# A pooled-attention and GELU kernel: denominators moved ahead of outputs in the first batch, one load moved to another queue, last row tile in two column parts

## The chip, the core and the metric

One core of a Trainium2 chip. The metric is the device time of one execution in microseconds (us), some 1.8 us longer than the span of the core's own instructions, which is what the profile shows. Engines in the profile: PE is TensorE, DVE VectorE, ACT ScalarE, POOL the gpsimd engine, SP the sync engine. Kernels are compared only within the same rounds. Ratios are the mean time of one kernel's fast runs over that of the other's of the same rounds, so not quite the ratio of the medians that are quoted; the range in brackets after a ratio is its 95% interval. Where a landing is given as a sum, it is the time of issue plus the time from issue to landing.

## The reference, cut to what matters

```python
# q, k, v: [8 batches, 8 heads, 576 rows, 64]; float32
k_p = k.reshape(B, H, 72, 8, D).mean(axis=3)         # pooled by 8
v_p = v.reshape(B, H, 72, 8, D).mean(axis=3)
attn = softmax(scale * q @ k_p^T)                    # over the 72 pooled rows
x = (attn @ v_p).transpose(0, 2, 1, 3).reshape(4608, 512)
out = gelu_tanh(x @ w_in) @ w_out                    # w_in 512 x 2048, w_out 2048 x 512
```

## The kernel before

Batch 0's attention runs alone. After that, tokens are handled in 9 groups of 512: first projection with w_in (16 blocks of 4 matmuls, each followed by a GELU on ACT), then second projection with w_out (4 row tiles of 16 matmuls), in which the scores and outputs of the next batch are put in between. Matmul operands are bfloat16. The loads of w_in, w_out and q cast from float32 and are issued by the gpsimd engine; batch 1's k and v go the same way, without a cast. One queue, in this order:

```python
    load_k(0, [nc.sync, nc.scalar])
    load_v(0, [nc.sync, nc.scalar])
    load_q(0, 0, 1); load_q(0, 1, 2)          # gpsimd queue from here on
    ...
    load_w_in(0); load_w_in(1)
    load_k(1, [nc.gpsimd])
    load_q(1)
    load_v(1, [nc.gpsimd])                    # two halves: heads 0-3 to partitions 0-63, heads 4-7 to 64-127
    for i in range(4): ...                    # w_out in four quarters
```

The end of batch 0's attention. `den0` sums exponentials on PE, `inverse0` makes 1/sum on ACT, `av0` is the output product on PE, `mult0` scales it on DVE; the last argument is the first of the banks used of PSUM, the memory that matmuls write to. `spin` issues matmuls on zeros, results unused, which keep PE busy while it waits for ACT and DVE:

```python
    inverse0(1, 0, 6)
    spin(4, 4)
    av0(0, 0, 4); mult0(0, 0, 4)
    den0(0, 2, 2); inverse0(0, 2, 2)
    av0(1, 0, 0); mult0(1, 0, 0)
    spin(3, 6)
    den0(1, 2, 6); inverse0(1, 2, 6)
    spin(3, 4)
    av0(0, 2, 4); mult0(0, 2, 4)
    spin(3, 0)
    av0(1, 2, 0); mult0(1, 2, 0)
    for fo, ko in [(fo, ko) for ko in range(2) for fo in range(4)]:
        p1_mm(0, fo, ko)                      # group 0's first projection starts
```

In group 0, work for batch 1 hangs on the blocks of the first projection; `kk` are the sums over k on DVE, `tq` the four groups of q's transposes on PE, `tk` k's transposes, `vv` the sums over v. Then each row tile of the second projection is copied out of PSUM and stored with four DMAs:

```python
    plan = {0: kk, 12: tq[:1], 13: tq[1:2] + tk, 14: tq[2:3], 15: tq[3:] + vv}
    ...
    nc.vector.tensor_copy(out=osb, in_=PS[:, o_bank(g, r), :])
    for n in range(4): ...                    # 32 rows each; on sync, every other one on scalar for the last tile
```

The softmax here doesn't subtract the row's maximum and nothing guards it: scores larger than these inputs give would overflow.

## Time and profile before

| | before |
|---|---|
| device time, median of 4 | 309.03 us (308.62 to 309.35) |
| the profiled execution | 308.29 us, span 306.5 us |
| PE busy | 298.2 us, 97% of the span |
| ACT, DVE, POOL busy | 71%, 49%, 12% |
| HBM read, written | 36.70 MB, 9.44 MB |

PE is busy nearly throughout, so a gain must shorten PE's work, a wait of PE, or what follows its last matmul. The profiled execution was faster than any of the timed ones. The prediction shows the views that carry this.

### The profile page before, as it was taken

Reading aid. Unit: us, or ns where it says so; the run is one execution under the profiler, and the core shown is the slowest. Engines: PE = TensorE matmul, PEld = TensorE weight load, DVE = VectorE, ACT = ScalarE, POOL = GpSimd, SP = SyncE. Lnnn points to the kernel's source line nnn. Section 1 sums busy time; section 2 is a strip of 40 time slices with the busy share of each in tenths; the row PEclk is TensorE's granted clock in tenths of the full one; section 3 lists DMA queues with packets and bytes.
Section 4 is the critical chain, followed back from the end, with each engine's and each line's share of the span. In section 5 each row is a group of like instructions: output and inputs, shape, how many; then the busy total and the mean of one; then the engine's idle time right before and its main releaser. Section 6 shows DMA issues by size and latency. Waiting matters only on the chain.

```text
span 306.5 us, 4325 instructions
## 1 busy us (share of the span) xinstructions
PE 298.2 (97%) x1518; PEld 157.4 (51%) x1548; DVE 150.4 (49%) x334; ACT 219.0 (71%) x402; POOL 36.3 (12%) x69
## 2 busy tenths in 40 slices
PE   8999999999999999999999999999999999999994
PEld 3555555555555555555555555555555555445441
DVE  5868557573677057806681559245933630110021
ACT  1686679868987798779977998789868987206400
POOL 7103002305004000220014000400000000000000
PEclk9999999999999999999999999999999999999999
DMA  7999996987957952596159725662101210121022
GB/s 225 266 257 253 214 186 137 299 176 177 269 146 167 247 122 51 114 282 156 34 112 266 168 56 106 200 151 71 35 1 36 63 41 2 34 70 34 2 70 68
DMA packets 30359, 41.12 MB, mean 134 GB/s; under 512 B 18113, under 2 KB 18113, under 8 KB 29441
## 3 DMA queue, kind: packets, MB, share of 16 engines
q0 software_dynamic: 7856, 25.43, 34.9%
q1 hardware_dynamic: 21888, 14.09, 19.2%
q10 hardware_dynamic: 592, 1.31, 1.2%
q8 instruction: 12, 0.20, 0.3%
q14 instruction: 11, 0.08, 0.1%
HBM read 36.70 MB, written 9.44 MB: 151 GB/s over the span
## 4 chain that ended last, share of the span: by engine, by line
PE 83%; DMA 12%; POOL 1%; issue 1%; ACT 0%; DVE 0%; POOLq 0%
PE PS L345 38%; PE PS L336 36%; DMA kt<-in_k_dram 7%; DMA w_out_b<-in_moe_w_out_dram 5%; PE PS L239 4%; PE PS L261 4%; PE PS L174 1%; POOL w_in_b L105 0%; POOL qb L86 0%; POOL w_out_b L113 0%; DVE osb L350 0%; ACT e L247 0%; ACT ld L269 0%; ACT ld L268 0%; POOL identb masks.py:199 0%
## 5 line engine op out<-in xcount | busy, mean ns | idle before, releaser
L345 PE MATMUL PS<-w_out_b,gT 128*128 128x512 bf16 x560 | 134.2, 379 | 0.9
L336 PE MATMUL PS<-xT,w_in_b 128*128 128x512 bf16 x563 | 126.2, 379 | 0.6
L342 ACT ACTIVATE gT<-PS 128x512 bf16<-128x512 f32 x144 | 81.1, 604 | 47.5 <-PE PS L336 47.4
L336 PEld LDWEIGHTS <-w_in_b 128*128 128x128 bf16 x576 | 64.7, 113 | 57.2
L345 PEld LDWEIGHTS <-gT 128*128 128x128 bf16 x576 | 56.1, 97 | 56.7 <-issue 1.1
L350 DVE COPY osb<-PS 128x512 f32<-128x512 f32 x36 | 24.9, 691 | 98.3 <-PE PS L345 95.3
L279 DVE TENSOR_TENSOR xT<-PS,rc 64x288 bf16<-64x288 f32 x112 | 51.0, 455 | 31.6 <-ACT rc L271 29.3
L247 ACT ACTIVATE e<-PS 72x576 bf16<-72x576 f32 (+1 forms) x64 | 41.0, 646 | 9.1 <-PE PS L239 8.2
L239 PE MATMUL PS<-qT,kT 128*72 128x288 bf16 (+1 forms) x128 | 25.9, 286 | 0.9 <-ACT qT L214 0.6
L271 ACT ACTIVATE rc<-ld 128x288 f32<-128x288 f32 x56 | 24.8, 443 | 1.8
L314 ACT ACT_TABLE_LOAD x17 | 21.8, 1283 | 4.3 <-issue 4.1
L268 ACT ACTIVATE ld<-PS 64x288 f32<-64x288 f32 x56 | 22.8, 407 | 1.3
L269 ACT ACTIVATE ld<-PS 64x288 f32<-64x288 f32 x56 | 22.5, 402 | 1.3
L261 PE MATMUL PS<-e,vp 72*128 72x288 bf16 (+1 forms) x112 | 23.1, 286 | 0.0
L139 DVE TENSOR_TENSOR kt<-kt 128x1280 f32<-128x1280 f32 (+5 forms) x18 | 18.8, 1044 | 5.5 <-DMA kt<-in_v_dram 2.6
L239 PEld LDWEIGHTS <-kT 128*72 128x72 bf16 (+1 forms) x128 | 13.2, 105 | 15.2 <-DVE qT L216 1.2
L448 POOL COPY gate<-qT 1x2 bf16<-1x2 bf16 x6 | 1.0, 174 | 140.0 <-DMA qT<-qb 140.0
L139 DVE TENSOR_TENSOR vt<-vt 128x1024 f32<-128x1024 f32 (+1 forms) x16 | 15.3, 956 | 1.8 <-DMA vt<-in_v_dram 1.5
L184 DVE COPY kT<-PS 64x288 bf16<-64x288 bf16 (+2 forms) x48 | 13.0, 319 | 6.2 <-PE PS L174 6.1
L362 PE MATMUL PS<-idle 128*128 128x512 bf16 x39 | 11.9, 447 | 1.2 <-DVE idle L127 1.2
L261 PEld LDWEIGHTS <-vp 72*128 72x128 bf16 (+1 forms) x112 | 11.0, 98 | 3.8
L81 POOL DMA_DIRECT2D vt<-in_v_dram x14 | 9.0, 655 | 7.5 <-DMA w_in_b<-in_moe_w_in_dram 5.5
(47 smaller groups left out, 90.0 us busy)
## 6 DMA issues: line engine op xcount, KB each, us to landing
out_dram<-osb SPq DMA_DIRECT2D x142, 64.0 KB
kt<-in_k_dram POOLq DMA_DIRECT2D x7, 1024.0 KB, 6.2
vt<-in_v_dram POOLq DMA_DIRECT2D x14, 512.0 KB, 8.6
qb<-in_q_dram POOLq DMA_DIRECT2D x7, 576.0 KB, 11.6
w_in_b<-in_moe_w_in_dram POOLq DMA_DIRECT2D x2, 1024.0 KB, 16.7
w_out_b<-in_moe_w_out_dram POOLq DMA_DIRECT2D x4, 512.0 KB, 13.9
kt<-in_k_dram POOLq DMA_DIRECT2D x7, 128.0 KB, 5.9
kt<-in_v_dram POOLq DMA_DIRECT2D x14, 64.0 KB, 5.7
```

The lines of the kernel that those rows point to most:

```text
L139: nc.vector.tensor_tensor(out=o, in0=a, in1=b, op=ALU.add)
L239: nc.tensor.matmul(out=PS[:n, bank + e, :CH].rearrange("j (t p) -> j t p", p=32), lhsT=kTs[b % 2][c][:, h, :n], rhs=qTs[b][:, h // 4, :, h ...
L247: nc.scalar.activation(out=e[:n], in_=PS[:n, bank:bank + 2, :CH], func=ACT.Exp, scale=1.0 / 64.0)
L261: nc.tensor.matmul(out=PS[:, bank + x, :CH], lhsT=window(vps[b % 2][:n], 2 * pr + x), rhs=e[:n, x, :], start=True, stop=True)
L268: nc.scalar.activation(out=ld[0:64], in_=PS[64:128, bank, :CH], func=ACT.Ln)
L269: nc.scalar.activation(out=ld[64:128], in_=PS[0:64, bank + 1, :CH], func=ACT.Ln)
L271: nc.scalar.activation(out=rc, in_=ld, func=ACT.Exp, scale=-1.0)
L279: nc.vector.tensor_tensor(out=xT[rows, pr, col:col + CH], in0=PS[rows, bank + x, :CH], in1=rc[rows], op=ALU.mult)
L336: nc.tensor.matmul(out=PS[:, h_bank(g, fo), c0:c1], lhsT=w_in_b[fo // 8][:, ko, q * 512 + j:(q + 1) * 512:4], rhs=xT[:, ko, r0 + c0:r0 + c ...
L342: nc.scalar.activation(out=gTs[g][:, fo, :], in_=PS[:, h_bank(g, fo), :], func=ACT.Gelu_apprx_tanh)
L345: nc.tensor.matmul(out=PS[:, o_bank(g, r), :], lhsT=gTs[g][:, fo, r * 128:(r + 1) * 128], rhs=w_out_b[:, fo, :], start=(fo == 0), stop=(fo ...
L350: nc.vector.tensor_copy(out=osb, in_=PS[:, o_bank(g, r), :])
```

## The change

Three parts. The later denominators go ahead of the outputs, so that ACT gets them sooner and fewer zero matmuls are needed (six for thirteen in the stretch shown). Batch 1's v goes to the sync queue, issued after a one-column memset of its tile on DVE that follows the first product; so it moves beside w_in, k and q instead of behind them. The last row tile is computed, copied and stored in columns 0:384 and then 384:512.

```diff
-    load_v(1, [nc.gpsimd])
...
-    spin(4, 4)
+    spin(2, 4)
+    den0(0, 2, 2)
+    inverse0(0, 2, 2)
+    spin(2, 4)
     av0(0, 0, 4)
     mult0(0, 0, 4)
-    den0(0, 2, 2)
-    inverse0(0, 2, 2)
+
+    nc.vector.memset(vts[1][:, 0, 0:1], 0.0)
+    load_v(1, [nc.sync])
+    den0(1, 2, 6)
+    inverse0(1, 2, 6)
     av0(1, 0, 0)
     mult0(1, 0, 0)
-    spin(3, 6)
-    den0(1, 2, 6)
-    inverse0(1, 2, 6)
-    spin(3, 4)
     av0(0, 2, 4)
     mult0(0, 2, 4)
-    spin(3, 0)
+    spin(2, 0)
...
-        seq = [(r, fo) for r in range(4) for fo in range(FO)]
+        seq = [(r, fo) for r in range(4 if g + 1 < NG else 3) for fo in range(FO)]
...
+    for c0, c1, bank in ((0, 384, o_bank(g, 3)), (384, DM, 4)):
+        for fo in range(FO):
+            p2_mm(g, 3, fo, bank, c0, c1)
+        store(g, 3, bank, c0, c1)
```

More of the change, by code (lines that the diff above doesn't have):

```diff
@@ L342, in gelu, with p2_mm, store @@
         nc.scalar.activation(out=gTs[g][:, fo, :], in_=PS[:, h_bank(g, fo), :], func=ACT.Gelu_apprx_tanh)
-    def p2_mm(g, r, fo):
-        nc.tensor.matmul(out=PS[:, o_bank(g, r), :], lhsT=gTs[g][:, fo, r * 128:(r + 1) * 128], rhs=w_out_b[:, fo, :],
-                         start=(fo == 0), stop=(fo == FO - 1))
-    def store(g, r):
-        osb = opool.tile([128, DM], F32, name="osb")
-        nc.vector.tensor_copy(out=osb, in_=PS[:, o_bank(g, r), :])
+    def p2_mm(g, r, fo, bank, c0=0, c1=DM):
+        nc.tensor.matmul(out=PS[:, bank, c0:c1], lhsT=gTs[g][:, fo, r * 128:(r + 1) * 128],
+                         rhs=w_out_b[:, fo, c0:c1], start=(fo == 0), stop=(fo == FO - 1))
+    osbs = {}
+    def store(g, r, bank, c0=0, c1=DM):
+        if (g, r) not in osbs:
+            osbs[g, r] = opool.tile([128, DM], F32, name="osb")
+        osb = osbs[g, r]
+        nc.vector.tensor_copy(out=osb[:, c0:c1], in_=PS[:, bank, c0:c1])
         for n in range(4):
-            b, c = divmod(g * GROUP + r * 128 + n * 32, S)
+            b, col = divmod(g * GROUP + r * 128 + n * 32, S)
             rows = out[b * S:(b + 1) * S].rearrange("(p t e) d -> e t p d", t=TP, e=2)
-            eng = nc.scalar if (g, r) == (NG - 1, 3) and n % 2 else nc.sync
-            eng.dma_start(out=rows[c // CH, c % CH // 32], in_=osb[n * 32:(n + 1) * 32, :])
+            eng = nc.scalar if c1 - c0 < DM and n % 2 else nc.sync
+            eng.dma_start(out=rows[col // CH, col % CH // 32, :, c0:c1], in_=osb[n * 32:(n + 1) * 32, c0:c1])
     def spin(n, bank):
@@ L519 @@
                 f(*a)
-            p2_mm(g, r, fo)
+            p2_mm(g, r, fo, o_bank(g, r))
             if fo == FO - 1:
-                store(g, r)
+                store(g, r, o_bank(g, r))
         for m in sorted(todo):
```

## The prediction

> **What bounds the kernel now.** I read the page first: busy shares, then the slices. TensorE (PE) carries the span.
>
> ```profile
> PE 298.2 (97%) x1518; PEld 157.4 (51%) x1548; DVE 150.4 (49%) x334; ACT 219.0 (71%) x402; POOL 36.3 (12%) x69
> ...
> PE   8999999999999999999999999999999999999994
> ...
> PEclk9999999999999999999999999999999999999999
> ```
>
> PE has no slack from the second slice to the last one, and its clock is granted in full. So time is saved only by taking instructions off PE, by removing a wait that PE still has, or by shortening what follows its last matmul. The change touches two stretches, about 16 to 45 us and the end, so I read those closely. First PE's timeline where the zero matmuls (line 362) stand:
>
> ```profile
> 15.98 1.03 PE L362 MATMUL PS<-idle 128*128 128x512 bf16 x4
> 17.18 0.66 PE L304 MATMUL PS<-e,vz 72*128 72x288 bf16 x4 [0.17 <-DVE vz L139]
> 17.68 0.66 PE L289 MATMUL PS<-e,ones 128*128 128x288 bf16 x4
> 18.17 0.66 PE L304 MATMUL PS<-e,vz 72*128 72x288 bf16 x4
> 18.66 0.81 PE L362 MATMUL PS<-idle 128*128 128x512 bf16 x3
> 19.31 0.65 PE L289 MATMUL PS<-e,ones 128*128 128x288 bf16 x4
> 19.80 0.81 PE L362 MATMUL PS<-idle 128*128 128x512 bf16 x3
> 20.45 0.65 PE L304 MATMUL PS<-e,vz 128*128 128x288 bf16 x4
> 20.94 0.81 PE L362 MATMUL PS<-idle 128*128 128x512 bf16 x3
> 21.59 0.65 PE L304 MATMUL PS<-e,vz 128*128 128x288 bf16 x4
> 22.08 0.38 PE L336 MATMUL PS<-xT,w_in_b 128*128 128x512 bf16 x1
> ```
>
> Starts are what counts, as matmuls overlap: three zero matmuls advance PE by 0.65 us (18.66 to 19.31), 0.216 each; four 288-column ones by 0.49. The zero matmuls fill time in which ScalarE and VectorE make the denominators and products; the first real projection starts at 22.08.
>
> Next, the chain that ended last, in order of time. Before group 0's second projection it is no PE chain but a DMA chain:
>
> ```profile
> 27.46 16.53 DMA w_out_b<-in_moe_w_out_dram
> 43.99 0.04 issue
> 44.03 0.81 PE PS L345 x3
> ```
>
> The last quarter of w_out lands at 43.99 and PE starts at once. Counting from the block that starts at 42.94, the fifth matmul (the first that needs this quarter) was due at 42.94 + 4 x 0.216 = 43.80, so PE waited 0.2 us. The block at 40.94 hides a like 0.2 us (its six matmuls take 1.51 us where 1.29 is due). Loading and PE are thus within 0.2 us of each other here: **PE time saved before 44 us is worth nothing unless w_out comes earlier.** That is the main question. The DMA view, two us of the startup, four us while batch 1's v moved, and four of w_out alone:
>
> ```profile
> q10 hardware_dynamic: 124, 0.25, 35.5%
> ...
> q0 software_dynamic: 239, 0.85, 105.8%
> ...
> q0 software_dynamic: 233, 0.84, 104.5%
> ```
>
> Columns are packets, MB and share of the 16 engines' time. The first row is ScalarE's hardware queue from 11 to 13 us, when only batch 0's v was left on it: 0.25 MB in 35.5% of 2 us is 352 GB/s of engine time. The second is the gpsimd queue from 29 to 33 us with batch 1's v in it: 0.85 MB in 4.23 us of engine time is 201 GB/s, like the casting w_out load of the third row (37 to 41 us), though v is not cast. In the software queue v costs the engines as much as a casting load. The engines are full from 3 to 45 us.
>
> **What the Trainium skill says.** "TensorE: Matmul & The Clock Gate", section "Back-to-back issue gap", gives N/2.4 + 2.5 ns warm, 216 ns for 512 columns and 56 for 128. The trace agrees: 0.216 above, and five 128-column transposes at 33.30 advance PE by 0.28 us. "DMA: Bandwidth & Descriptors", section "Issuing engines are not separate DMA queues", says that another issuing engine saves only sequencer time, as all share 16 engines. The trace does not quite agree: 352 against 201 GB/s for the same kind of v load. The same page, "Queues, rings and completion order", says that each DMA engine serves its queues in turn, packet by packet. It agrees with 5 to 13 us, where the three queues moved about 100 packets each in every two us. So v on the sync queue will not wait behind w_in, k and q; it will slow them.
>
> **Part 1, the order and seven zero matmuls fewer.** Thirteen of them follow 15.98 in four blocks (4, 3, 3, 3); the change keeps six (2, 2, 2). By PE time: 7 x 0.216 = 1.51 us. What of it becomes waiting? I put the new order on the old durations. Two zeros end at 16.41; the denominators (their second exponential was done by 15.7) to 16.90; two zeros to 17.33; outputs (0,0) to 17.83 (vz ready at 17.12, so the 0.17 us wait is gone); denominators (1,2) to 18.32; outputs (1,0) to 18.81. VectorE multiplies (0,0) from about 18.0 to 18.8 (0.76 each), does a tiny memset, and multiplies (1,0) until about 19.8. Outputs (0,2) need the banks of the first product: 18.9 to 19.4. The last two zeros write the bank that (1,0)'s product reads, so they wait until 19.8: 0.4 us idle. Then 0.43 to 20.25 and 0.49 to **20.75**. The third product ends at 20.5 and the fourth, whose inverse ScalarE ends at about 20.8, at 21.6, before the ninth projection matmul needs it (20.75 + 8 x 0.216 = 22.5). So the projection starts 22.08 - 20.75 = **1.33 us** earlier. The first half of w_in landed by 17.5 (3.04 + 14.2 by its tile view), so it does not hold this.
>
> **Part 2, v on the sync queue.** The issue follows the memset, near 19.0, and bytes flow from about 20.1 (1.1 us after issue, as at the start). v is 1.05 MB: at 352 GB/s 3.0 us of engine time, at the old 201 to 213 about 5. So w_out, behind it in both cases, lands about 2 us earlier: 43.99 to about 42.0. PE will want the last quarter at 43.80 - 1.33 = 42.5. The DMA bound goes, and with it the 0.4 us of waiting. But what lay before v is now delayed by up to 3.0 us: the second half of w_in from 23.0 (3.8 + 19.2) to at most 25, wanted at 20.75 + 32 x 0.216 = 27.7, harmless; k from 26.1 to about 28.8, where VectorE gets to it at 28.4 now and PE transposes the result only at 34.67, harmless. And batch 1's q:
>
> ```profile
> DMA to landing us min/median/max: 7.1/9.1/21.7
> ```
>
> This is the q tile's view up to 25 us, three loads; the slowest is batch 1's, issued at 8.59, so it lands at 30.3. PE transposes it at 33.30 now and wants it at 31.97 then. With 2 to 3 us added it lands at 32.3 to 33.3: I choose 32.8, a new wait of **0.8 us**. So this stretch keeps 1.33 - 0.8 + 0.4 = **0.9 us** (0.4 to 1.75). From then on PE is dense, and the gain goes through to the end.
>
> **Part 3, the last tile in columns 0:384 and 384:512.** The end now:
>
> ```profile
> 302.11 0.69 DVE L350 COPY osb<-PS 128x512 f32<-128x512 f32 x1 [2.76 <-PE PS L345]
> 302.83 0.78 SPq L356 DMA_DIRECT2D out_dram<-osb  x2
> 302.84 0.85 ACTq L356 DMA_DIRECT2D out_dram<-osb  x2
> ```
>
> Sixteen more matmuls, but the same columns: 16 x (0.162 + 0.056) against 16 x 0.216 is +0.03 us. The last copy has 128 columns: 0.69 is 0.53 at one element a cycle of 0.96 GHz plus 0.16, so 0.13 + 0.16 = 0.29, saving 0.40. The first part's copy (0.56) and its four issues run from about 301.3 to 302.6, so the second part's can go out at about 302.5 to 302.65 instead of 302.83; with 16 KB instead of 64 KB each the last landing comes 0.4 to 0.7 us earlier. I take **0.5 us**. "VectorE: DVE Perf Modes", section "Why PSUM operands drop a tier", keeps float32 from PSUM at one element a cycle, which 0.69 us for 512 columns fits.
>
> **Sum.** 0.9 + 0.5 = 1.4, and a little for the chance that q comes in time: 1.6 us. 309.19 - 1.6 = 307.6 us.
>
> **Rivals.** (a) Loading stays the bound: v costs 5 us on the sync queue too, w_out still lands at 44.0. For it: full DMA engines and the skill's sentence. Against it: 352 GB/s on the hardware queue. Then the start gives about 0.1 and the end 0.5: 308.6. (b) q comes in time, because v takes fewer turns before it: the start gives 1.33 + 0.4, the whole 2.2: 307.0. (c) The new order makes ScalarE or the banks the wait, and PE idles for the removed zeros; 1.33 falls to 0.5 or less, but then q's wait shrinks as well: about 308. (d) Less activity lowers the PE clock; gaps of 0.4 us beside a dense stream speak against it, and I give it little.
>
> **Range and chances.** Rival (a) and the three runs before (308.62 to 309.35) set the upper edge, 308.8; (b) with some noise the lower, 306.7. Two per cent is 6.2 us, over three times the best sum and far from any loss I can find: faster 0.01, same 0.98, slower 0.01.
>
> **What would show it.** First projection matmul near 20.75; PE waiting up to 1.3 us at the transposes of batch 1's q after 13 of the 16 blocks; last quarter of w_out before 42.5 and no wait on it; batch 1's v on the sync queue at some 350 GB/s; last copy near 0.29 us, and about 3.9 us instead of 4.4 (306.5 - 302.1) from the last matmul to the span's end. A q wait above 1.5 us, w_out still at 44, or a projection start after 21.5 would make me wrong; so would a slower dense part.

## The result

The changed kernel took 307.45 us (median of 4, 306.73 to 307.9) against 309.03; ratio 0.9947, 95% interval 0.9924 to 0.9971. That is the same within 2%, and 1.6 us faster. A second measurement (below) gave 307.13 against 309.04, ratio 0.9942.

The profile of the changed kernel, in the order of the prediction. PE's timeline over the reordered stretch (start us, us, engine, line, operation, operands, count; in brackets what PE waited for):

```profile
16.11 0.59 PE L365 MATMUL PS<-idle 128*128 128x512 bf16 x2
16.54 0.65 PE L288 MATMUL PS<-e,ones 128*128 128x288 bf16 x4
17.03 0.59 PE L365 MATMUL PS<-idle 128*128 128x512 bf16 x2
17.46 0.66 PE L303 MATMUL PS<-e,vz 72*128 72x288 bf16 x4
17.95 0.66 PE L288 MATMUL PS<-e,ones 128*128 128x288 bf16 x4
18.44 1.24 PE L303 MATMUL PS<-e,vz 72*128 72x288 bf16 x8
20.02 0.59 PE L365 MATMUL PS<-idle 128*128 128x512 bf16 x2 [0.34 <-DVE xT L307]
20.45 0.65 PE L303 MATMUL PS<-e,vz 128*128 128x288 bf16 x4
20.94 1.24 PE L335 MATMUL PS<-xT,w_in_b 128*128 128x512 bf16 x5
```

The order is as worked out, with one wait of 0.34 us for the product that reads the bank of the last zeros (0.4 predicted). The projection starts at 20.94 (20.75 predicted) instead of 22.08. What comes before this stretch also varies from trace to trace, so the better measure counts from the first zero matmul: 22.08 - 15.98 = 6.10 us before, 20.94 - 16.11 = 4.83 after, 1.27 us less.

Next, 13 blocks later, batch 1's q. The chain that ended last, cut off at 45 us:

```profile
8.79 24.89 DMA qb<-in_q_dram
33.68 0.05 issue
33.73 0.45 PE PS L203 x5
```

q was issued at 8.79 and landed at 33.68, 3.4 us later than before (30.3). PE's timeline shows the wait in its bracket:

```profile
33.73 0.34 PE L203 MATMUL PS<-identb,qb 128*128 128x128 bf16 x3 [1.41 <-DMA qb<-in_q_dram]
```

So PE, 1.14 us early at 20.94, comes out of this 0.43 us late (33.73 against 33.30). Then it no longer waits for w_out, and where it reaches the next batch's fourth pair of score matmuls it is exactly where it was: first line before, second the changed kernel.

```profile
44.68 0.41 PE L239 MATMUL PS<-qT,kT 128*128 128x288 bf16 x2
```

```profile
44.67 0.41 PE L238 MATMUL PS<-qT,kT 128*128 128x288 bf16 x2
```

From there both traces run alike up to the last matmul. In this pair of traces the start gave **nothing**, and what remains is the end:

```profile
301.25 0.56 DVE L353 COPY osb<-PS 128x384 f32<-128x384 f32 x1 [1.91 <-PE PS L344]
301.84 1.80 ACTq L359 DMA_DIRECT2D out_dram<-osb  x4
302.15 0.29 DVE L353 COPY osb<-PS 128x128 f32<-128x128 f32 x1 [0.34 <-PE PS L344]
```

The last copy is 0.29 us instead of 0.69, and the span ends at 306.1, 3.95 us after it starts instead of 4.39 (306.5 - 302.11): 0.44 us. But the timed gain is 1.6 us, not 0.4. The profiled execution of before was its fastest (308.29), that of the changed kernel its slowest (307.9). One pair of traces does not settle where 1.6 us come from; the experiments had to.

### The profile page after: what moved, and what is told of

Read it like the earlier page. It is cut to its first block, busy times and chain, and to the rows that moved or that the text cites. A ratio compares the mean times of both kernels' runs of the same rounds, so it can differ in the third digit from the quotient of the medians.

```text
span 306.1 us, 4354 instructions
## 1 busy us (share of the span) xinstructions
PE 296.8 (97%) x1528; PEld 157.6 (51%) x1557; DVE 150.5 (49%) x336; ACT 219.0 (72%) x402; POOL 35.0 (11%) x67
## 3 DMA queue, kind: packets, MB, share of 16 engines
q0 software_dynamic: 7568, 24.38, 33.7%
q1 hardware_dynamic: 22528, 15.14, 21.1%
## 4 chain that ended last, share of the span: by engine, by line
PE 87%; DMA 11%; issue 1%; ACT 0%; DVE 0%; POOLq 0%
PE PS L344 40%; PE PS L335 37%; DMA qb<-in_q_dram 11%; PE PS L238 5%; PE PS L260 4%; PE PS L173 1%; PE PS L203 0%; ACT e L246 0%; ACT ld L268 0%; ACT ld L267 0%; DVE osb L353 0%; POOLq L550 0%
## 5 line engine op out<-in xcount | busy, mean ns | idle before, releaser
L344 PE MATMUL PS<-w_out_b,gT 128*128 128x512 bf16 (+2 forms) x577 | 133.9, 373 | 0.7
L344 PEld LDWEIGHTS <-gT 128*128 128x128 bf16 x592 | 57.0, 97 | 55.7 <-issue 0.4
L353 DVE COPY osb<-PS 128x512 f32<-128x512 f32 (+2 forms) x37 | 25.1, 677 | 98.2 <-PE PS L344 78.6
L267 ACT ACTIVATE ld<-PS 64x288 f32<-64x288 f32 x56 | 22.8, 408 | 1.3
L365 PE MATMUL PS<-idle 128*128 128x512 bf16 x32 | 10.4, 468 | 1.6 <-DVE idle L126 1.2
L76 POOL DMA_DIRECT2D kt<-in_v_dram x14 | 8.0, 586 | 0.1
```

Source lines behind the costliest of these rows:

```text
L267: nc.scalar.activation(out=ld[0:64], in_=PS[64:128, bank, :CH], func=ACT.Ln)
L344: nc.tensor.matmul(out=PS[:, bank, c0:c1], lhsT=gTs[g][:, fo, r * 128:(r + 1) * 128], rhs=w_out_b[:, fo, c0:c1], start=(fo == 0), stop=(fo ...
L353: nc.vector.tensor_copy(out=osb[:, c0:c1], in_=PS[:, bank, c0:c1])
```

## The experiments

Each ran on one chip beside the kernel before, mostly in five rounds. Theory A: the start is bound by loading, and the parts help only together. Theory B: the removed zero matmuls are the gain. Theory C: only the end is real.

### The parts alone

**Order alone**: the hunk between `inverse0(1, 0, 6)` and the projection, without its two v lines; `load_v(1, [nc.gpsimd])` stays.

> Order and six zero matmuls instead of thirteen alone; v stays on the gpsimd queue, last tile whole. Theory A (the start is bound by loading): the projection starts near 21.0 us as in the changed kernel, batch 1's q lands near 30.3 and is not waited for, but w_out's quarters still land near 36.6 to 44.0 and PE now waits for them, about 1.3 us in all; PE reaches the work after 44.7 us at the same time as before, and the kernel gains 0 to 0.2 us. Theory B (PE's own instructions bound it, the removed zero matmuls are gained): 1.2 to 1.5 us faster. Theory C (the tail is all of the gain): 0.

Measured: 308.79 us against 309.23, ratio 0.9996 (0.9974 to 1.0018). PE's timeline of group 0's second projection:

```profile
36.54 1.47 PE L345 MATMUL PS<-w_out_b,gT 128*128 128x512 bf16 x6 [0.17 <-DMA w_out_b<-in_moe_w_out_dram]
...
39.05 1.45 PE L345 MATMUL PS<-w_out_b,gT 128*128 128x512 bf16 x6 [0.37 <-DMA w_out_b<-in_moe_w_out_dram]
```

The projection starts at 21.11, q is not waited for, and w_out lands as before (its last quarter at 27.7 + 16.2 = 43.9): PE waits for it, here with brackets that the kernel before did not have. Theory B wanted at least 1.2 us; the interval allows 0.8. It falls.

**v alone**: v's two lines in the old order, after `mult0(0, 0, 4)`; the gpsimd load removed.

> Batch 1's v on the sync queue alone, gated by the same memset after the first product, everything else as before. Theory A: q lands near 33.5 and PE, which comes to it at 33.3, waits 0.2 to 0.4 us; the last quarter of w_out lands near 43.5 instead of 44.0, so the 0.4 us of waits for w_out fall away; sum 0 +-0.3 us. Theory B and C: 0 as well, or a loss of 0.4 us. What it tells apart is in the trace: how much earlier w_out lands when v leaves the gpsimd queue and PE does not change.

Measured: 308.74 against 309.23, ratio 0.998 (0.9963 to 0.9997). That is 0.6 us, more than I expected, with an interval of 0.1 to 1.1. In its trace q landed at 33.9 (8.83 + 25.1) and w_out's last quarter at 44.0 (28.5 + 15.5); the projection started late, at 22.82, and PE waited for neither. w_out did not land earlier here. Counted from the first zero matmul, PE reaches the fourth pair of score matmuls after 28.26 us instead of 28.70, so the 0.4 us of waits for w_out are gone. But the last-tile version below, with v still on the gpsimd queue, needs 28.25: it too came to this stretch late (projection at 22.59), when w_out was there. So this trace shows nothing that moving v alone gains, and why the median is better than zero stays open.

**The last tile alone**:

> Only the last row tile in two column parts. My step: 0.4 to 0.5 us faster, the last copy 0.29 us instead of 0.69, the time from the last matmul to the span's end about 4.0 instead of 4.4 us. Theory C says that this is all that is real in the whole change, and everything beyond it noise. Rival: nothing, as the number of issues doubles.

Measured: 308.56 against 309.23, ratio 0.9981 (0.9965 to 0.9997): 0.6 us, the expected size (the interval is 0.1 to 1.1). In its trace the last copy takes 0.29 us and the span ends 3.8 us after that copy starts, against 4.4 before.

**All but the move of v**:

> The change without the move of v. Theory A: order and tail without earlier w_out, so 0.4 to 0.7 us faster than before, the start giving at most 0.2. Theory B: 1.7 to 2.0 us faster, better than the whole change, since q then lands at 30.3 and is not waited for. Theory C: 0.4 to 0.5.

Measured: 309.05 against 309.23, ratio 0.9993 (0.9974 to 1.0012). Theory B's 1.7 to 2.0 us falls again. In its trace PE waits 1.33 and 0.32 us for w_out, whose last quarter landed at 45.1 (27.3 + 17.8), late even for this kernel:

```profile
37.81 1.47 PE L345 MATMUL PS<-w_out_b,gT 128*128 128x512 bf16 x6 [1.33 <-DMA w_out_b<-in_moe_w_out_dram]
```

### The changed kernel again

> The changed kernel unaltered, with five rounds, beside three versions of it. The parts alone gave 0.1 (order), 0.6 (v) and 0.6 us (tail), and order and tail together 0.2; if the move of v lifts the load bound under the order (theory A), the whole gives more than the order and tail together: 1.0 to 1.7 us. If the first result was a lucky draw, 0.6 to 0.9. The trace: q lands near 33.5 and PE waits 1.0 to 1.6 us for it.

Measured: 307.13 us (306.73 to 308.2) against 309.04, ratio 0.9942 (0.9921 to 0.9962): 1.9 us. Theory C (0.5 us) falls, and so does the thought of a lucky draw. Its profiled execution took 306.73 us, and its trace is the other half of the story. PE's timeline at the first zero matmuls, where q's transposes start, and at the score matmuls that stood at 44.67:

```profile
16.44 0.59 PE L365 MATMUL PS<-idle 128*128 128x512 bf16 x2
...
32.52 0.45 PE L203 MATMUL PS<-identb,qb 128*128 128x128 bf16 x5
...
43.46 0.41 PE L238 MATMUL PS<-qT,kT 128*128 128x288 bf16 x2
```

No bracket: q landed at 32.5 (8.62 + 23.9), just as PE came. w_out's last quarter landed at 42.6 (26.6 + 16.0), in time. The view of the tile of w_out gives this landing; the shortest of its four is the last quarter's:

```profile
DMA to landing us min/median/max: 16.0/18.8/23.9
```

The same kernel keeps 1.2 us of its start (44.68 - 43.46) in this execution and none in the first, by when q lands: 1.2 us later there. With the end's 0.44 this is the whole span difference, 306.5 to 304.9.

So order, v and end together give 1.6 to 1.9 us, order and end without v 0.2: the order pays only when v is moved as well. That is theory A. The times alone would not settle it: the three parts timed singly sum to 1.3 us with wide intervals, and no version with v and end but without the order was run. The traces do settle it. From the first zero matmul to the fourth pair of score matmuls PE needs, in us:

| | old order | new order |
|---|---|---|
| v on the gpsimd queue | 28.70 (before), 28.25 (last tile alone) | 28.27 (order alone), 29.44 (all but v) |
| v on the sync queue | 28.26 (v alone) | 28.56 (first trace), 27.02 (this one) |

Traces in which PE waits for no load need 28.25 in the old order and 26.99 in the new (the version without v's load, below). So the order's 1.27 us is there in full only with v moved and q in time. With v on the gpsimd queue waits for w_out eat it; with v moved and q late the wait for q does. What follows this stretch, the end included, differs by at most 0.7 us over all traces. Full order and end come to 1.27 + 0.44 = 1.7 us by the traces; 1.6 and 1.9 were timed. Each cell has only one or two traces.

### What v costs

Batch 1's v isn't loaded; DVE zeroes its tile near 4 us.

```diff
+    nc.vector.memset(vts[1], 0.0)             # among the first memsets
...
     nc.vector.memset(vts[1][:, 0, 0:1], 0.0)
-    load_v(1, [nc.sync])
```

> The changed kernel without batch 1's v load at all: its tile is zeroed by VectorE in the idle time near 4 us, so the output of batch 1 is wrong on purpose. It measures what v costs. If v on the sync queue takes as long as the prediction had it (3.0 us), w_out's last quarter lands near 40.0 to 40.5 (42.5 to 43.5 minus 3); if it takes as long as on the gpsimd queue (5 us), near 38.5 to 39. q lands at 30.3 or before in both, PE waits for neither, the start keeps its full 1.3 to 1.8 us: 0.3 to 1.0 us faster than the changed kernel, near its fastest execution.

Measured: wrong (relative error 0.35), 306.38 us against 309.06, ratio 0.9911. w_out's last quarter landed at 39.3 (26.2 + 13.1):

```profile
DMA to landing us min/median/max: 13.1/15.5/20.8
```

Against 43.5 and 42.6 in the two traces of the changed kernel, v on the sync queue costs 3.3 to 4.2 us of loading, between my 3.0 and 5. With the trace of v alone (44.0) it is 4.7. On the gpsimd queue (43.9 to 44.0 in three traces, 45.1 in the fourth) it costs 4.6 to 4.7, and 5.8 in the fourth. The ranges touch, and only one trace lacks v: that v is cheaper on the sync queue is likely, not shown. Without q's wait and with w_out early, the kernel is some 0.9 us faster than the changed one. This is what the wait for q and late loads still cost on the mean, as far as kernels of different rounds can be compared.

When v moves is as telling. Packets, MB and share of 16 engines by queue in the changed kernel (first trace), from 19 to 22.8 us and then from 22.8 to 26.8:

```profile
q0 software_dynamic: 342, 1.07, 108.9%
q8 instruction: 1, 0.02, 1.5%
```

```profile
q0 software_dynamic: 197, 0.77, 64.5%
q1 hardware_dynamic: 195, 0.40, 39.0%
```

The sync engine issued v at 19.03, but its queue (q1) has no packet before 22.8. In five other traces with v on a hardware queue, issued anywhere from 19.4 to 30.6 us, its first packet comes 3.8 to 3.9 us after the issue as well; why is open. From then on the two queues take turns one for one (195 and 197 packets). v moves at 0.40 MB in 39% of 4 us, 256 GB/s of engine time, not 352. It falls beside k and q instead of beside w_in.

### Can q's wait be taken away?

**v's halves on two queues**, in case the halves, one for each half of the partitions, slow each other in turn:

```diff
-    load_v(1, [nc.sync])
+    load_v_half(1, 0, nc.sync)
     den0(1, 2, 6)
+    load_v_half(1, 1, nc.scalar)
     inverse0(1, 2, 6)
```

> The changed kernel with v's two halves on two hardware queues (sync and scalar) at the same place, instead of one after the other on sync. Each half goes to one half of the partitions, so that in turn they may use only half of the engines' write paths. If that is what makes v slow (theory P), w_out's last quarter lands 1 us or more earlier than in the changed kernel (43.5), near 42.3, and q near 32.5 instead of 33.7; the kernel gains 0.5 to 1.0 us on the changed one. If not, q and w_out land as in the changed kernel and the time is the same.

Measured: 307.39 against 309.04, ratio 0.9946, as the changed kernel; q at 33.2 (9.13 + 24.1), waited for 0.24 us; w_out's last quarter at 43.0 (27.4 + 15.6). Theory P isn't supported on the hardware queues. Why v is slow on the gpsimd queue stays open, but it is not that queue alone: batch 1's k, not cast either, moved on it in the kernel before at 0.43 MB in 104.5% of one us (22 to 23 us), 411 GB/s of engine time. (That this is k follows from the order of the loads and its packets of 8 KB.) k goes to all 128 partitions in runs of 8 KB, each half of v to 64 in runs of 2 KB; which of the two matters was not tested.

**v behind k's sums**:

```diff
-    nc.vector.memset(vts[1][:, 0, 0:1], 0.0)
-    load_v(1, [nc.sync])
...
+            if g == 0:
+                kk.append(lambda: (nc.vector.memset(vts[1][:, 0, 0:1], 0.0), load_v(1, [nc.sync])))
             kk.append(lambda: v_moves(nb))
```

> The changed kernel with v's gate behind batch 1's k sums on VectorE (near 31.5 us) instead of behind the first product (19 us), so that v moves beside w_out and no longer beside k and q. If the wait for q comes from v going ahead of it (theory A), q lands near 30.3 and PE, there at about 31.9, does not wait; w_out's last quarter lands at 42.5 to 43.5 and PE waits 0 to 1 us for it; 0.4 to 1.2 us faster than the changed kernel. If q is late for another reason, the wait stays.

Measured: 316.25 against 309.04, ratio 1.0229: my gain turned into 7.2 us of loss. Half of the expectation held: q landed at 29.8 (8.75 + 21.0) and was not waited for, w_out's last quarter at 41.2 (26.9 + 14.3). But v was issued at 30.61, and the first output product of batch 1 waited for its sums:

```profile
47.86 0.66 PE L260 MATMUL PS<-e,vp 72*128 72x288 bf16 x2 [7.65 <-DVE vp L138]
```

v takes turns with the gpsimd queue (59 packets against 63 from 40 to 41 us), and its sums start only at 45.40. The wait has a second price: the granted clock is 1.00 up to 44 us, 0.57 from 44 to 48, 0.58 from 48 to 52 and 1.00 after that, and the four 512-column matmuls at 49.16 advance PE by 0.43 us each instead of 0.216. From the first zero matmul to the fourth score pair it takes 36.52 us, 9.5 more than the changed kernel's best; 7.65 is the wait, the rest fits the low clock. What this shows for theory A: q's wait does come from v going ahead of it.

**Both**, v's second half on scalar behind the twelfth GELU (`plan` gets `11: [lambda: load_v_half(1, 1, nc.scalar)]`, the sync half gated as in the last one):

> Both: v's halves on sync (gated behind the k sums) and on scalar (behind the twelfth GELU), so both near 31.5 us. Theory P and A together: no wait for q, w_out's last quarter before 42.5, no wait for it, 1.0 to 1.6 us faster than the changed kernel. Without P as v_after_k_sums. The issue on scalar costs ScalarE 0.7 us among the GELUs, where it has 0.27 us of slack in each 0.87; if that is too much, the second projection starts late.

Measured: 314.63, ratio 1.0174. The wait is 5.19 us instead of 7.65. A miss for the same reason, less so as the two queues together get two turns out of three (39, 39 and 38 packets from 38 to 39 us). Here too the clock falls, to 0.50 from 44 to 48 us.

**q's transposes one block later**:

```diff
-    plan = {0: kk, 12: tq[:1], 13: tq[1:2] + tk, 14: tq[2:3], 15: tq[3:] + vv}
+    plan = {0: kk, 13: tq[:1], 14: tq[1:2] + tk, 15: tq[2:] + vv}
```

> The changed kernel with the transposes of batch 1's q one projection block (0.86 us) later. If the wait for q is the loss and varies between executions (0 in one trace, 1.4 us in the other), the later place takes up to 0.86 us of it: 0.3 to 0.6 us faster on the mean, less spread. If the gain went elsewhere, the same time as the changed kernel.

Measured: 307.75 against 309.06, ratio 0.9966 (0.9941 to 0.9991): not faster than the changed kernel. q's wait is gone, but DVE gets to v's sums later, as they follow the copies of these transposes, and a new wait stands at the same output product:

```profile
40.88 0.42 PE L260 MATMUL PS<-e,vp 72*128 72x288 bf16 x2 [0.59 <-DVE vp L138]
```

Two of its six executions also had a granted clock of 0.994 and 0.989 and took 308.8 and 309.6 us; the others took 307.2 to 307.9.

**v's halves on two queues, in the middle**: after the memsets of k's tiles on DVE, and behind the second GELU.

```diff
-    nc.vector.memset(vts[1][:, 0, 0:1], 0.0)
-    load_v(1, [nc.sync])
...
     nc.vector.memset(kTs[1][1], 0.0)
+    nc.vector.memset(vts[1][0:64, 0, 0:1], 0.0)
+    load_v_half(1, 0, nc.sync)
...
-    plan = {0: kk, 12: tq[:1], 13: tq[1:2] + tk, 14: tq[2:3], 15: tq[3:] + vv}
+    plan = {0: kk, 1: [lambda: load_v_half(1, 1, nc.scalar)], 12: tq[:1], ...}   # the rest as it was
```

> The changed kernel with v's halves on sync (gated among VectorE's memsets near 23 us) and scalar (behind the second GELU, near 25 us), so that its first packets, some 3.9 us after the issue, come near 27 to 29 us, and v moves beside q and the first quarter of w_out. q then lands near 31.5 to 32 and is waited for 0 to 0.3 us; v is there by 36 to 37, when VectorE sums it; w_out's last quarter near 43. 0.2 to 0.8 us faster than the changed kernel. If v is late again, PE waits for it at the first output product of batch 1 and the kernel is slower.

Measured: **306.66 us** (306.48 to 306.95) against 309.06, ratio 0.9922 (0.9905 to 0.9939). q lands at 30.1 (9.04 + 21.1), w_out's last quarter at 42.4 (26.4 + 16.0), PE waits for neither:

```profile
32.32 0.44 PE L207 MATMUL PS<-identb,qb 128*128 128x128 bf16 x5
...
43.25 0.41 PE L242 MATMUL PS<-qT,kT 128*128 128x288 bf16 x2
```

This beats the kernel before, and has the lower median of the two changed versions (306.66 against 307.13, not run side by side; the intervals overlap). Its five executions lie within 0.5 us where the changed kernel's six lie within 1.5. That this is because q no longer decides is not shown: the two-queue version at the old place, in whose trace PE did wait for q, lies within 0.5 too.

**Both of the last two**:

> Both of the last two. No wait for q is left; w_out's last quarter (43) is 0.5 us late for PE (42.4) at most: 0.4 to 1.0 us faster than the changed kernel, and the fastest of all, if nothing else comes up.

Measured: 308.02, ratio 0.9977 (0.9947 to 1.0007), a miss. The new wait of 0.59 us for v's sums is there again, and three of six executions had a granted clock of 0.989 or 0.994 (308.45 to 309.91 us). Transposing later is the wrong cure. The lower clock has a likely cause. Both versions with v after k's sums show 0.984 to 0.989 in all their executions, and their traces put it from late in PE's long wait for v's sums to 3 to 5 us after it; these two versions wait for the same sums. A longer wait in just those executions would do it, but they were not profiled, so this is not shown.

## Why the prediction was right, and where it wasn't

The time (307.6 predicted, 307.45 and 307.13 measured), the range and the class held. By its steps:

- **Start of the projection, 1.33 us earlier.** Right: 1.27. From the first zero matmul to the projection it is 6.09 to 6.10 us in all three traces of the old order and 4.82 to 4.83 in all eleven of the new. (The starts themselves, 1.14 us apart in the first pair, also carry the scatter of what comes before.) The predicted idle of 0.4 us is there, at 0.34.
- **"PE time saved before 44 us is worth nothing unless w_out comes earlier."** Right, and shown: the order alone gave 0.1 us, order and end without v 0.2, all three 1.6 to 1.9, and the table above has the waits. The bound holds for an execution that comes early, as the one I read; in the trace of the last tile alone, half a microsecond later, no load was waited for.
- **"bytes flow from about 20.1 (1.1 us after issue, as at the start)".** Wrong: none before 22.8, 3.8 us after issue. At the start (first issue at 0.74, first packets between 1.7 and 1.9) the engines had been idle. So w_in was hardly slowed, and k and q took the turns.
- **v costs 3.0 us of engine time.** Too small: 3.3 to 4.7. The rate of 352 GB/s came from a stretch in which the gpsimd queue's packets were 2.0 KB on average; beside k and q they were 3.9 KB, and v's rate was 256. That the packets are the reason is not shown. So w_out's last quarter came at 42.6 to 43.5 instead of 42.0; in neither trace of the changed kernel did PE wait for it.
- **q's wait, 0.8 us** (landing at 32.8). The mechanism was right, the landing scatters: 33.7 with a wait of 1.4, 32.5 with none. The single number lay between by luck. My sentence that it could be as little as none (rival b) and as much as 1.3 described it better than the number did. In the five traces with v issued near 19 us, q landed at 32.5 to 33.9.
- **k harmless.** Right for PE, though DVE had to wait for it: its sums began at 30.00 instead of 28.40.
- **The end, 0.5 us.** Right: 0.44 in the trace, 0.6 timed. The copies of 512, 384 and 128 columns took 0.69, 0.56 and 0.29 us, 1.04 ns a column plus 0.16 us, as the prediction had split it.
- **Two readings of the evidence.** "The three queues moved about 100 packets each in every two us" from 5 to 13 us holds only from 9 to 11 (103, 102, 102); in the other windows one queue moved 44 to 66. The turns are better shown by the changed kernel (197 and 195). And the section cited for N/2.4 + 2.5 ns ("Back-to-back issue gap") gives that formula for an isolated matmul, and about 131 ns for a stream of 512 columns. The streams in these traces advance by 216 ns (six matmuls of the second projection in 1.30 us, 37.61 to 38.91 in the changed kernel), so the formula fits and the section's figure for streams doesn't.
- **Sum.** 0.9 for the start: 0 and 1.2 in the two traces; on the mean about 1.1 to 1.3, if the end's 0.6 is taken off 1.7 to 1.9.

Of the rivals, (a) lives on in half: with v on the gpsimd queue loading is the bound as soon as PE comes early. (b) is what the one fast execution with a trace did. (c) and (d) had nothing in the traces of the changed kernel, beyond the 0.34 us of idle that was predicted (clock 1.000 and 0.998); the clock did fall where PE waited for 5 to 8 us in other versions.

## What to carry to other kernels

Where loads and compute arrive within tenths of a microsecond of each other, shortening compute gives nothing until the loads are reordered too, so test the parts together and without each one. A load moved to another queue does not wait behind the others any more but took turns with them here (197 packets against 195): issue it so late that what has the nearer deadline is already through, and so early that its own turns suffice; here 19 us made q late, 31 us made v late, 23 to 25 us, on two queues, suited both. Measure a stretch from a mark close before it, not from the start of the trace: here the start of the projection scattered by 0.7 to 0.9 us within one order, but counted from the first zero matmul the two orders differ by 1.26 to 1.28 us in every pair. And compare several traces of one kernel when the gain is near the scatter: one pair here said 0.4 us where the timing said 1.6.

## What the Trainium skill lacked or had wrong

- "DMA: Bandwidth & Descriptors", section "Latency and other measured facts", gives about 600 ns to the first byte of a load issued on a hardware queue. With the engines full of the gpsimd queue's loads, no byte of the sync queue's load moved before 3.8 us after its issue (19.03 to 22.8), and 3.8 to 3.9 us in five more traces. For a busy chip the section has only an HBM access latency (2 us at high load), no first-byte figure.
- The same page, "Issuing engines are not separate DMA queues", says that another issuing engine saves only sequencer time. Here choosing the queue also chose the order: q landed at 32.5 to 33.9 us in the five traces with v on a hardware queue from 19 us on, and at 29.7 to 30.3 in the four with v on the gpsimd queue. The same load may also have cost less, 3.3 to 4.7 us of loading against 4.6 to 5.8, judged by when the last quarter of w_out landed with and without it; the ranges touch, so this is not shown.
- No page says why v, which isn't cast, runs on the gpsimd queue at the 201 GB/s of a casting load while k, not cast either, runs there at 411. Two hardware queues for v's halves changed nothing (ratio 0.9946 against 0.9942), so it stays open.
